# All tiles in SBUF on multiples of 64 bytes: a bias tile and a carried tile widened, 32 bytes left out at the upper end

## The chip, the cores and the metric

The kernel runs on one core of a Trainium2 chip. The metric is the device time of one execution in microseconds; three runs of the kernel before gave 2819.92, 2820.65 and 2821.26 us. A profile of one execution comes with it: for each engine (PE is TensorE, DVE is VectorE, ACT is ScalarE, POOL is GpSimd, SP issues most of the DMAs) each instruction's start and duration, and what released it when it had waited.

## The reference

A Fourier layer over 8 sequences of 3008 positions with 256 channels, followed by a gated feed-forward network over all 24,064 tokens:

```python
X = np.fft.rfft(x, axis=1)
Yr = Xr @ w_r - Xi @ w_i + b_r
Yi = Xr @ w_i + Xi @ w_r + b_i
Yr = np.sign(Yr) * np.maximum(np.abs(Yr) - lam, 0.0)   # lam = 0.01
Yi = np.sign(Yi) * np.maximum(np.abs(Yi) - lam, 0.0)
y = np.fft.irfft(Yr + 1j * Yi, n=x.shape[1], axis=1)
...
gate = 1.0 / (1.0 + np.exp(-(y @ w_gate)))
return gate * (y @ w_val) @ w_out                      # 256 -> 1536 -> 256
```

## The kernel before

**Staging.** The transform is split into two steps with 47 and 64 points. For each batch, `fwd_a` (its matmul is line 176) does the first step, its result goes through DRAM, `fwd_b` (line 237) does the second, `mix` or `mix4` (lines 271 and 293) multiplies by the complex weights, `inv_b` (lines 305 to 310) begins the inverse, again through DRAM, and `inv_a` (line 340) ends it. The feed-forward network then runs in two ways. The first nine chunks of 512 tokens go one after another: for each of 12 blocks of the hidden width, `ffn1` (lines 399 to 401) makes gate and value, and `ffn2` (lines 427 to 429), two blocks behind, multiplies by `w_out`. The FFT of the later batches is done between these units. The other tokens are taken in 19 pairs of 512 after the last FFT; for them the first layer is done by a scheme with seven products in place of eight (`product`, line 659), and `second` (lines 634 to 636) does the last layer. One pass through `half` has seven such products, three matmuls each, and one hidden block of `second` for both halves of the pair, twelve matmuls.

**Operands.** Most matmuls take float32 values as a high part and a low part of fewer bits: `yth` and `ytl` are the two parts of the transform's result for a chunk, `hh` and `hl` those of the gated hidden values, `w1h` and `w1l` those of the first layer's weights, and `w2` holds both parts of the last layer's. A product is then three matmuls (high by high, low by high, high by low). In a row of the profile, `po<-hh,w` means the result `po` from the moving operand `hh` and the stationary weights `w`.

**Memory.** Tiles come from pools that lie on two stacks in each partition of SBUF. From the left: `const` (`fb_sb`, `w1h`, `w1l`, `w2`), `cw` (`fa_sb`, `w_sb`, `bias_sb`, `ebias`), and `p2` (the FFT's working tiles, such as `xsh`, `xsl`, `yh`, `yl`, `zf`, `mi_sb` and, at the start, the warm-up tile `zero`). When the FFT is over, `cw` and `p2` are closed, and `p4` takes their place: `th` and `tl` (weights of the seven-product scheme), ten slots `xop` for its moving operands (`a11`, `s1` and so on; three of them serve as `spare` for the last hidden blocks of the first nine chunks), `ypair` and `sop`. From the right: `p0` (first batch), in whose place comes `p3` (`vf`, `yth`, `ytl`, `carry`, `sg`, `hh`, `hl`, and `ry` for results), in whose place comes `p5` (temporaries `tmp`, the hidden parts `hp`, results `ot2`). A pool's tiles stand one behind the other, and each tile takes a multiple of 32 bytes. The tile `carry` holds what `inv_a` computes beyond the end of a chunk until the next one begins; `ebias` is a column of one constant that ScalarE adds while the weights, given as 64-bit floats, are brought to 32 bits.

In the program before, `const` starts at byte 16,512 of a partition and the right stack ends at byte 229,344. `ebias` is the last tile of `cw`, at 105,472 and 32 bytes wide, so `p2` starts at 105,504. `carry` is 1504 bytes wide, at 205,312; right of it stand `sg`, `hh`, `hl` and `ry`, left of it `ytl`, `yth` and `vf`.

**Order.** The start is written out by hand up to the end of the twelve first units; after that the side work is put between units by weights. No queue and no order is touched by the change.

Of the kernel before, what the change touches and what calls it, by code (L numbers as in the profile page):

```python
# [9 lines left out]
F32 = mybir.dt.float32  # L10
# [99 lines left out]
def tile_fft_mix_ffn(ctx: ExitStack, tc, x, w_r, w_i, b_r, b_i, w_one, w_out, mf, mi, mis, fa, fb, out):  # L110
# [3 lines left out]
    P = 128  # L114
    XR = x.shape[2]
    CT = D // P
# [4 lines left out]
    UT = 2 * PT  # L121
# [6 lines left out]

    const = ctx.enter_context(tc.tile_pool(name="const", bufs=1))

    p0s = ExitStack()
    p0 = p0s.enter_context(tc.tile_pool(name="p0", bufs=1, side="right"))
    p3s = ExitStack()
    fft = ExitStack()
    cw = fft.enter_context(tc.tile_pool(name="cw", bufs=1))
# [5 lines left out]
    def bank(name, tag="fft", bufs=FFT_BANKS):  # L141
        return (psf if tag == "fft" else psl).tile([P, 512], F32, tag=tag, bufs=bufs, name=name)
# [185 lines left out]
    def split_y(c, at, n, y):  # L328
        if c not in yts:
            yts[c] = [p3.tile([P, CT, CW], F32R, name=t) for t in ("yth", "ytl")]  # L330
        yh, yl = (t[:, :, at:at + n] for t in yts[c])
        nc.scalar.copy(yh, y)
        sub(yl, y, yh)

    def inv_a(u):
        vf = held.pop(("v", u))
        pa = bank("pia")[:, :CT * UT].rearrange("p (c h k) -> p c h k", c=CT, h=2)
        for hh in range(2):
            for ct in range(CT):
                nc.tensor.matmul(pa[:, ct, hh], vf[:, hh, ct * P:(ct + 1) * P], fb_sb[:, :PT], start=True, stop=True)  # L340
        py = pa.rearrange("p c h k -> p c (h k)")
        lo = u * UT
        n = 0
        if lo < T0:
            c, at = divmod(lo, CW)
            n = min(UT, CW - at)
        if 0 < n < UT and lo + n < T0:
            t = p3.tile([P, CT, UT], F32, name="carry", bufs=1)[:, :, :UT - n]
            nc.scalar.copy(t, py[:, :, n:])
            held["carry", c + 1] = t, UT - n  # L350
        if n:
            split_y(c, at, n, py[:, :, :n])
        if lo + UT > T0:
            t = result("yf")
            t = t[:, :CT * (UT - n)].rearrange("p (c k) -> p c k", c=CT)
            nc.scalar.copy(t, py[:, :, n:])
            nc.sync.dma_start(yd[:, :, lo + n - T0:lo + UT - T0], t)

    def result(name):
        return p3.tile([P, CW], F32, tag="ry", bufs=NYF, name=name)  # L360
# [123 lines left out]
    def ffn_units():  # L484
        units, todo = [], {}
        seq = [(c, f) for c in range(NPL) for f in range(NF)]

        def own(c):

            return range(-(-c * CW // UT), -(-(c + 1) * CW // UT))  # L490

        for c in range(1, NPL):
            at = (c - 1) * NF
            for i, u in enumerate(own(c)):
                todo.setdefault(at + (0, 3, 6)[i], []).append(lambda u=u: load_v(u))
                todo.setdefault(at + (3, 6, 9)[i], []).append(lambda u=u: inv_a(u))
            todo.setdefault(at + 1, []).append(lambda c=c: carry(c))

        def unit(n):
            c, f = seq[n]  # L500
            if n == 0:
                for i, u in enumerate(own(0)):
                    if i == 1:
                        w = w1h[:, 0].rearrange("p i t n -> p (i t n)")
                        keep_warm(bank("warm", "l1", L1_BANKS), w[:, :P], w, WARM_V)
                    inv_a(u)
            ffn1(c, f)
            for t in todo.pop(n, ()):
                t()
            if n >= LAG and n - LAG < len(seq) - BEHIND:  # L510
                ffn2(*seq[n - LAG])
        return [lambda n=n: unit(n) for n in range(len(seq))], own(0), own(NPL - 1)[-1] + 1
# [228 lines left out]

    bias_sb = cw.tile([P, 2, D], F32, name="bias_sb")
    bias4 = p0.tile([P, D], F32, name="bias4")
    ebias = cw.tile([P, 1], F32, name="ebias")
    fb_sb = const.tile([2 * NQ, P], F32, name="fb_sb")
    w1h = const.tile([P, NF, 2, CT, P], F32R, name="w1h")
    w1l = const.tile([P, NF, 2, CT, P], F32R, name="w1l")
# [183 lines left out]
    p3 = p3s.enter_context(tc.tile_pool(name="p3", bufs=2, side="right", reuse_waits="tile"))  # L931
# [18 lines left out]
    def inverse(g):  # L950

        us = [u for b in g for u in range(b * H // 2, (b + 1) * H // 2) if u >= u0]
        ahead = min(NVF - 1, len(us))

        def begin():
            for u in us[:ahead]:
                load_v(u)

        def go(i):
            if i + ahead < len(us):  # L960
                load_v(us[i + ahead])
            inv_a(us[i])
        return [(0.0, begin)], [(0.65, lambda i=i: go(i)) for i in range(len(us))]

    def behind(g):

        loads, units = inverse(g)
        return (loads, 0.05, 0.05), (units, 0.1, 1)

    def merge(*streams):  # L970

        return [u for _, _, u in sorted(((lo + (hi - lo) * (i + 0.5) / len(s), k, u) for k, (s, lo, hi) in
                                         enumerate(streams) for i, u in enumerate(s)), key=lambda t: t[:2])]

    (a3, q3), (a4, q4) = (fft_units(g, {}) for g in groups[3:])
    n = len(a3) // 3
    side = (merge((second_fft, 0, 1), (a3[:n], 0.2, 1)) +
            merge((third_fft, 0, 1), (a3[n:], 0, 0.85), *behind(groups[1])) +
            merge((q3, 0, 1), (a4, 0, 0.85), *behind(groups[2])) +
            merge((q4, 0, 1), *behind(groups[3])))  # L980
# [9 lines left out]
    for j in range(NF, len(ffn)):  # L990
        c, f = divmod(j, NF)
# [39 lines left out]
    a, b, c, d = banks[0]  # L1031
# [4 lines left out]
    with tc.manual_schedule():  # L1036
        for k in range(2 * NPR * NH):
            p, e = divmod(k, 2 * NH)
# [18 lines left out]
        n = NPR * NH  # L1057
# [36 lines left out]
```

## Time and profile before

| | |
|---|---|
| median of three runs | 2820.65 us |
| span of the profiled execution, first to last instruction | 2819.0 us |
| TensorE busy | 2802.4 us |
| VectorE busy | 2082.3 us |
| ScalarE busy | 1309.6 us |
| GpSimd busy | 710.5 us |
| moved by DMA | 241.01 MB, 85 GB/s over the span |

The profile gives the profiled execution's own time as its span. It is one execution; the runs were taken without a profile, and their median is 1.65 us more than the span.

A row of the groups gives the line, the engine, the operation, output and inputs by the program's names, the shape of the tile, and the count; behind the first bar the busy time of the group in us and the mean duration of one in ns; behind the second the time that the engine was idle just before these instructions, and what ended most of it. Matmuls overlap: the next one starts before the last one is out, so a matmul that is said to take 389 ns follows the one before it at a shorter step. The time of a row of matmuls is read from the difference of two starts in the timeline.

### The profile page before, as it was taken

The page shows a single profiled execution, that of the slowest core. Times are in us where ns is not written, and L with a number is a line of the kernel's source. Part 1 is how long each engine was busy: PE and PEld are TensorE (multiplying, and loading weights), DVE is VectorE, ACT ScalarE, POOL GpSimd, SP SyncE. Part 2 cuts the span into 40 slices and gives each one's busy share as a digit, 9 for nine tenths or more (in the row PEclk, how much of TensorE's full clock was granted, in tenths as well). Part 3 has the DMA queues.
Part 4 walks back from the last instruction along what each step waited for, and adds up shares of the span by engine and source line. Part 5 has one row for each costly group of instructions (what it writes and reads, how often), then busy time and mean ns, then how long its engine had stood idle before and what let it go on. Part 6 is the DMA issues. An engine that isn't in the chain of part 4 may idle for free.

```text
span 2819.0 us, 38251 instructions
## 1 busy us (share of the span) xinstructions
PE 2802.4 (99%) x13896; PEld 2308.1 (82%) x13896; DVE 2082.3 (74%) x3109; ACT 1309.6 (46%) x2276; POOL 710.5 (25%) x638
## 2 busy tenths in 40 slices
PE   9999999999999999999999999999999999999999
PEld 6678888888899888888888888888888888888887
DVE  5777778667787536777777777777777777777776
ACT  4664544545455444444444444444444444444443
POOL 0211010224100002333333333333333343333321
PEclk9999999999999999999999999999999999999999
DMA  9866544666554661000000000000000000000000
GB/s 296 257 213 194 170 143 149 199 184 192 165 152 140 186 187 38 30 15 16 30 31 27 4 31 31 31 16 15 31 30 16 15 30 31 30 1 30 30 16 15
DMA packets 173469, 241.01 MB, mean 85 GB/s; under 512 B 14592, under 2 KB 124896, under 8 KB 173280
## 3 DMA queue, kind: packets, MB, share of 16 engines
q1 hardware_dynamic: 163776, 214.93, 24.8%
q0 software_dynamic: 9408, 23.60, 2.5%
q8 instruction: 110, 1.80, 0.3%
q14 instruction: 79, 0.65, 0.1%
q10 hardware_dynamic: 96, 0.04, 0.0%
HBM read 134.17 MB, written 104.33 MB: 85 GB/s over the span
## 4 chain that ended last, share of the span: by engine, by line
PE 94%; DVE 2%; DMA 2%; ACT 1%; issue 0%; SPq 0%; DVEq 0%; ACTq 0%
PE pd L659 11%; PE pa L659 11%; PE pc L659 11%; PE po L636 8%; PE po L635 8%; PE po L634 8%; PE pm L271 6%; PE pb L659 5%; PE pia L340 4%; PE pb L237 3%; PE pa L176 2%; PE pg L399 2%; PE pg L401 2%; PE pg L400 2%; PE pv L399 2%; PE pv L400 2%
## 5 line engine op out<-in xcount | busy, mean ns | idle before, releaser
L636 PE MATMUL po<-hl,w 128*128 128x512 f32 x912 | 362.5, 397 | 0.0
L635 PE MATMUL po<-hh,w 128*128 128x512 f32 x912 | 361.5, 396 | 0.0
L634 PE MATMUL po<-hh,w 128*128 128x512 f32 x912 | 360.8, 396 | 0.0
L718 POOL TENSOR_TENSOR c<-c,c 128x512 f32<-128x512 f32 x114 | 147.7, 1296 | 831.0 <-DVE c L714 640.1
L659 PE MATMUL pa<-a,w1h 128*128 128x512 f32 x912 | 284.0, 393 | 0.0
L659 PE MATMUL pc<-s,w1h 128*128 128x512 f32 x912 | 283.7, 392 | 0.0
L714 DVE TENSOR_TENSOR c<-u,pc 128x512 f32<-128x512 f32 x228 | 156.7, 687 | 114.7 <-PE pc L659 106.2
L689 DVE TENSOR_TENSOR u<-u,pb 128x512 f32<-128x512 f32 x228 | 155.3, 681 | 88.8 <-PE pb L659 62.6
L606 ACT CAST hh<-v 128x512 fp32r<-128x512 f32 x114 | 70.7, 620 | 306.2 <-DVE v L699 306.2
L636 PEld LDWEIGHTS po<-hl,w 128*128 128x128 f32 x912 | 171.5, 188 | 41.9
L634 PEld LDWEIGHTS po<-hh,w 128*128 128x128 f32 x912 | 172.0, 189 | 40.9
L635 PEld LDWEIGHTS po<-hh,w 128*128 128x128 f32 x912 | 171.0, 188 | 40.8
L659 PEld LDWEIGHTS pa<-a,w1h 128*128 128x128 f32 x912 | 171.2, 188 | 40.1
L659 PEld LDWEIGHTS pc<-s,w1h 128*128 128x128 f32 x912 | 171.0, 188 | 37.6
L610 POOL TENSOR_TENSOR hl<-c,hh 128x512 fp32r<-128x512 f32 x114 | 152.4, 1337 | 186.1 <-ACT hh L606 186.1
L271 PE MATMUL pm<-w_sb,xsh 128*128 128x256 f32 x1008 | 189.4, 288 | 1.4 <-ACT xf L177 1.1
L659 PE MATMUL pc<-s,w1l 128*128 128x512 f32 x456 | 177.5, 389 | 0.0
L659 PE MATMUL pa<-a,w1l 128*128 128x512 f32 x456 | 177.0, 388 | 0.0
L720 DVE TENSOR_TENSOR u<-u,pd 128x512 f32<-128x512 f32 x228 | 156.9, 688 | 24.5 <-DVE c L714 0.9
L693 DVE TENSOR_TENSOR v<-v,pc 128x512 f32<-128x512 f32 x228 | 156.6, 687 | 24.4 <-DVE v L691 0.5
L691 DVE TENSOR_TENSOR v<-u,pd 128x512 f32<-128x512 f32 x228 | 156.9, 688 | 24.0 <-DVE u L689 0.5
L685 ACT COPY u<-pa 128x512 f32<-128x512 f32 x228 | 133.7, 586 | 78.7 <-PE pa L659 78.6
(174 smaller groups left out, 6738.7 us busy)
## 6 DMA issues: line engine op xcount, KB each, us to landing
zf<-zd SPq DMA_DIRECT2D x96, 256.0 KB, 3.6
vf<-vd SPq DMA_DIRECT2D x128, 192.0 KB, 3.1
out_dram<-ot SPq DMA_DIRECT2D x93, 256.0 KB, 2.2
vd<-vz SPq DMA_DIRECT2D x84, 256.0 KB, 2.9
ypair<-yd SPq DMA_DIRECT2D x19, 1024.0 KB, 5.0
yd<-yf SPq DMA_DIRECT2D x103, 188.0 KB, 3.0
xf<-in_x_dram SPq DMA_DIRECT2D x48, 384.0 KB, 4.1
zd<-xf SPq DMA_DIRECT2D x44, 384.0 KB, 3.4
```

What stands on the lines that cost most here:

```text
L271: nc.tensor.matmul(o, l, r, start=(i == 0), stop=(i == len(mms) - 1))
L610: sub_(hl, h, hh)
L634: nc.tensor.matmul(o, wh, hh, start=(f == 0), stop=False)
L635: nc.tensor.matmul(o, wl, hh, start=False, stop=False)
L636: nc.tensor.matmul(o, wh, hl, start=False, stop=(f == NF - 1))
L659: nc.tensor.matmul(o, l, r, start=not more and l is wh and r is xh, stop=l is wl, skip_group_check=more)
L689: add(u, u, b)
L691: add(v, u, d)
L693: add(v, v, c)
L714: add(c12, u, c)
L718: nc.gpsimd.tensor_mul(c12, g12, c12)
L720: add(u, u, d)
```

## The change

Three edits, all in the sizes of tiles. A pool `edge` is opened on the right before all others and holds one tile of 8 floats (32 bytes), which nothing uses. `carry` is allocated with 384 floats (1536 bytes) in a partition in place of 2 x 188 (1504), and the old shape is taken as a view of it. `ebias` is allocated with 16 floats (64 bytes) in place of one, and its first column is used.

```diff
     const = ctx.enter_context(tc.tile_pool(name="const", bufs=1))
 
+    edge = ctx.enter_context(tc.tile_pool(name="edge", bufs=1, side="right"))
+    edge.tile([P, 8], F32, name="edge")
     p0s = ExitStack()
     p0 = p0s.enter_context(tc.tile_pool(name="p0", bufs=1, side="right"))
...
         if 0 < n < UT and lo + n < T0:
-            t = p3.tile([P, CT, UT], F32, name="carry", bufs=1)[:, :, :UT - n]
+            t = p3.tile([P, 3 * P], F32, name="carry", bufs=1)[:, :CT * UT].rearrange("p (c k) -> p c k", c=CT)[:, :, :UT - n]
             nc.scalar.copy(t, py[:, :, n:])
...
     bias4 = p0.tile([P, D], F32, name="bias4")
-    ebias = cw.tile([P, 1], F32, name="ebias")
+    ebias = cw.tile([P, 16], F32, name="ebias")[:, :1]
     fb_sb = const.tile([2 * NQ, P], F32, name="fb_sb")
```

## The prediction

> **What bounds the kernel.** I read the page first: span, busy shares, granted clock, the shares of the chain that ended last.
>
> ```profile
> span 2819.0 us, 38251 instructions
> ...
> PE 2802.4 (99%) x13896; PEld 2308.1 (82%) x13896; DVE 2082.3 (74%) x3109; ACT 1309.6 (46%) x2276; POOL 710.5 (25%) x638
> ...
> PEclk9999999999999999999999999999999999999999
> ...
> PE 94%; DVE 2%; DMA 2%; ACT 1%; issue 0%; SPq 0%; DVEq 0%; ACTq 0%
> ```
>
> TensorE is busy for 2802.4 of 2819.0 us at a granted clock of nine tenths or more in every slice, and it is 94% of the chain. All waiting together is 16.6 us. So the time moves only if matmuls follow each other faster, or if part of that 16.6 us goes. Next, the table by stage: stages cut at the end of the first FFT work, at the last FFN units and at the start of the long second part (lines 634 to 659).
>
> ```profile
> 0.00:120.00 120.00, 111.68 (x597) 0.99 0.90 278
> 120.00:450.00 330.00, 327.79 (x1855) 1.00 0.63 186
> 450.00:960.00 510.00, 508.28 (x3283) 1.00 0.55 166
> 960.00:1085.00 125.00, 124.99 (x682) 1.00 0.59 178
> 1085.00:2819.00 1734.00, 1729.64 (x7488) 1.00 0.07 23
> ```
>
> Columns are stage, length, TensorE busy (matmuls), granted clock, DMA share, GB/s. Half of the 16.6 us lies in the first 120 us, where the DMA share is 0.90; the last stage is 1734 us, TensorE alone, DMA at 0.07.
>
> **Part 1: what the change moves.** It adds and removes no instruction. I laid out both versions from the sizes in the code and the allocation of the program before, where the first constant tile starts at byte 16,512 of a partition and the right side ends at 229,344 = 3583 x 64 + 32. On the left, `ebias` takes 64 bytes instead of 32, so all tiles of `p2` go from 32 past a multiple of 64 to a multiple, up by 32. On the right, `edge` takes the top 32 bytes: `p0`, `p5` and the `sg`, `hh`, `hl`, `ry` part of `p3` move down by 32, onto multiples. `vf`, `yth` and `ytl` lay on multiples already; the wider carry tile and `edge` move them down by 64. `const`, the large tables of `cw` and all of `p4` stay. The gap between the sides shrinks from 1504 to 1408 bytes, so it fits.
>
> **Part 2: waits.** A pool that takes over another's bytes makes its tiles wait for those it overlaps. I compared the pairs `p4` over `cw`/`p2`, `p3` over `p0` and `p5` over `p3`: shifts of 32 bytes change no pair, since each boundary of one list keeps its side of the nearest boundary of the other. So no wait is added or taken away, nothing new queues behind anything, and no DMA is moved past another on SP's or POOL's queue. I price the waits at 0.
>
> **Part 3: the matmuls.** If addresses matter, the rows of equal matmuls from differently placed tiles must differ. These are 128x512 groups, shapes kept apart (last columns: busy us, mean ns, idle):
>
> ```profile
> L636 PE MATMUL po<-hl,w 128*128 128x512 f32 x912 | 362.5, 397 | 0.0
> L635 PE MATMUL po<-hh,w 128*128 128x512 f32 x912 | 361.5, 396 | 0.0
> L634 PE MATMUL po<-hh,w 128*128 128x512 f32 x912 | 360.8, 396 | 0.0
> ...
> L400 PE MATMUL pv<-ytl,w1h 128*128 128x512 f32 x216 | 85.5, 396 | 0.0
> ...
> L427 PE MATMUL po<-hh,w 128*128 128x512 f32 x210 | 84.8, 404 | 0.0
> ...
> L427 PE MATMUL po<-spare,w 128*128 128x512 f32 x6 | 2.3, 389 | 0.0
> ```
>
> The last two are the same line, weights and kind of bank; only the moving tile differs: `hh` lies 32 past a multiple of 64, `spare` (in `p4`) on one. 404 holds waits, but lines 634 to 636 wait for nothing and stand at 396 to 397. So the place of the moving tile goes with some 7 ns. The timeline shows what that costs in a row; start in us stands first. One of the 228 halves of the last stage (912 / 4):
>
> ```profile
> 2793.96 0.40 PE L634 MATMUL po<-hh,w 128*128 128x512 f32 x1
> ...
> 2796.78 0.63 PE L659 MATMUL pa<-a,w1h 128*128 128x512 f32 x2
> ...
> 2798.85 0.62 PE L659 MATMUL pa<-a,w1h 128*128 128x512 f32 x2
> ...
> 2801.57 0.40 PE L634 MATMUL po<-hh,w 128*128 128x512 f32 x1
> ```
>
> Twelve matmuls on `hh` and `hl` take 2796.78 - 2793.96 = 2.82 us, 235 ns from start to start. Twelve from `p4` later in the same half take 2801.57 - 2798.85 = 2.72 us, 226.7 ns. The nine in between (2.07 us, 230 ns) read `p4` too and come back to the short step only by and by. A half takes 7.61 us; 33 steps of 226.7 ns would be 7.48. The most that is to be had here is 228 x 0.13 = 29.6 us.
>
> The last FFN units, without side work:
>
> ```profile
> 1068.95 0.40 PE L427 MATMUL po<-hh,w 128*128 128x512 f32 x1
> ...
> 1069.65 0.39 PE L399 MATMUL pg<-yth,w1h 128*128 128x512 f32 x1
> ...
> 1072.45 0.63 PE L659 MATMUL pa<-a,w1h 128*128 128x512 f32 x2
> ```
>
> Twelve on `yth`/`ytl` take 2.80 us against 2.72: 0.08 x 108 units = 8.6 us. Three on `hh`/`hl` take 0.70 against 0.68: 0.02 x 2 x 105 = 4.2 us. With the last stage that makes a ceiling of 42.4 us.
>
> Now which property of the place it is. `yth` and `ytl` start on multiples of 64 (188,928 = 2952 x 64) and still step at 233 ns. And the warm-up tile `zero`, in `p2`, 32 past a multiple, in its last matmuls:
>
> ```profile
> L836 PE MATMUL warm<-zero x5: 388/389/393, 29.6 to 30.5; 128*128 128x512 f32 x5
> ```
>
> Least, median and longest: 389, the short value, off a multiple of 64. So the rows speak twice against "a multiple of 64 is what counts". Two properties fit all five tiles. (a) Distance to the weights, modulo 512: weight slices start at 128 past a multiple of 512, the operands of `p4` too (127,616), and `zero` is its own weight: distance 0, short. `yth` starts 128 short of that phase, `hh`/`hl` 160: long. After the change all of these stand at 192, a distance no 512-wide row shows. (b) Place in the partition: the long ones lie above 180,000, the short ones end at 168,576; nothing crosses over. Under (b) the change does nothing; under (a) it leaves distance 0 to the same tiles as before, and the new 192 is nearer to 160 and 128 (both long) than to 0 or 512. I take 0 for the sum, with -42.4 as the near end and a dearer pattern, below, as the other.
>
> The Trainium skill, page "SBUF — State Buffer", section "Door 1: The DMA port swizzle (why [64,N] ≈ [32,N])", says that SBUF has 16-byte lines and that crossing to a new one costs; tiles on multiples of 32 begin on such a line before and after, so by that rule alone the matmul term is 0, yet it leaves the 389 against 396 unexplained.
>
> **Part 4: the 256-wide matmuls of the FFT**, operands in `p2` and `cw`:
>
> ```profile
> L271 PE MATMUL pm<-w_sb,xsl 128*128 128x256 f32 x504 | 141.4, 281 | 0.0
> ...
> L293 PE MATMUL pm<-wi_sb,xsl 128*128 128x256 f32 x48 | 13.5, 281 | 0.0
> L293 PE MATMUL pm<-w_sb,xsl 128*128 128x256 f32 x48 | 13.4, 280 | 0.0
> ```
>
> `w_sb` lies on a multiple of 64 and `wi_sb` 32 off; they differ by 1 ns. Bounds: 1512 (line 271) x 1 ns = 1.5 us either way; I take 0.
>
> **Part 5: other engines and DMA.**
>
> ```profile
> L610 DVE TENSOR_TENSOR hl<-v,hh 128x512 fp32r<-128x512 f32 x114 | 79.0, 693 | 78.2 <-ACT hh L606 78.2
> ...
> L606 ACT CAST hh<-v 128x512 fp32r<-128x512 f32 x114 | 70.7, 620 | 306.2 <-DVE v L699 306.2
> ...
> L585 ACT CAST a<-ypair 128x512 fp32r<-128x512 f32 x57 | 34.9, 612 | 0.5 <-DMA ypair<-yd 0.5
> ...
> L416 DVE TENSOR_TENSOR spare<-sg,spare 128x512 fp32r<-128x512 f32 x3 | 2.1, 693 | 2.1 <-ACT spare L415 2.1
> ```
>
> VectorE takes 693 ns from tiles all 32 off and 693 where two of three are on a multiple; ScalarE 620 off against 612 on. At 46% ScalarE sits before it casts (306.2 us idle), so 8 ns times 456 casts, 3.6 us, lies beside TensorE's products: 0 on the path; if the cover went, 3.6 us at most. DMA: in the chain the longest piece is the first load of x.
>
> ```profile
> 3.18 10.38 DMA xf<-in_x_dram
> 13.57 8.18 DMA wf<-in_w_r_dram
> 21.83 7.47 DMA zd<-xf
> 33.16 6.18 DMA zf<-zd
> ```
>
> Together 32.2 us of transfers into or out of tiles that move by 32. No row shows the same load at both places, so bounds: 0, or a tenth of these 32.2 us, 3.2 us, either way; I take 0, as rows of 1 to 4 KB per partition are long against 32 bytes.
>
> Sum: 0 + 0 + 0 + 0 on a span of 2819.0 us. The median of the runs is 2820.65, 1.65 above the span; I keep that difference: 2820.7 us.
>
> **Rivals.**
> - *Distance 192 is as good as 0* (reading (a) with luck): every matmul of part 3 steps at 226.7 ns, -42.4 us, 2778 us. For: the sharp, exactly repeated short step. Against: 128 and 160 are both long. Chance 0.22.
> - *A multiple of 64 does count for `hh` and `hl`* and `yth` is long for a reason of its own: 29.6 + 4.2 = 33.8 us, 2787 us. For: `spare` against `hh` in line 427. Against: `zero` at 389. Chance 0.16.
> - *Slower: distance 192 gives a dearer pattern.* The dearest that recurs is line 636, most often 399 ns:
>
> ```profile
> L636 PE MATMUL po<-hl,w x912: 394/399/399, 1094.9 to 2814.6; 128*128 128x512 f32 x183
> ```
>
> If every 512-wide matmul on a moved tile took 399: 2736 x 2.7 ns on lines 634 to 636 = 7.4 us, 1296 x 3 on `yth`/`ytl` (396 on line 400) = 3.9, 630 x 3 on lines 427 to 429 = 1.9; 13.2 us, 2834 us. Its place is TensorE's operand reads; it decides from 5.6 us / 4662 matmuls = 1.2 ns each. Against: the mean is already 396. Chance 0.12.
> - *The change misses its aim* (a pool rounds its start, so that the tiles keep their places): 2820.7, within the forecast's case.
>
> **How the numbers follow.** No change (2815 to 2826, within 0.2%, about what a measurement of this kernel can tell from none): 0.50. Faster: 0.22 + 0.16 = 0.38. Slower: 0.12. The two faster cases are too likely to leave out, so the range reaches to 2777; above it ends at 2832, short of the full dearer pattern. That leaves about 0.1 out.
>
> **What would show it.** In the profile after: lines 634 to 636 stay at 394 to 399 and the half at 7.6 us if the forecast holds; 389 and 7.48 us under the first rival, with `yth` at 389 too; 389 there but `yth` at 393 to 395 under the second; 399 or more under the third. Lines 271 and 293 within 1 ns, the idle total near 16.6 us, no new releaser among TensorE's waits, else part 2 is wrong. I am wrong if the 512-wide means move by more than 1.2 ns without any of these patterns.

## The result, and the profile after

The changed kernel takes 2804.28 us (median of four runs, 2803.84 to 2806.39) against 2820.56 us before: ratio 0.9944, 95% interval 0.993 to 0.9958. It is 16.3 us faster, where no change was forecast, and inside the range. The page of the profiled execution (2804.69 us) begins so:

```profile
span 2802.9 us, 38251 instructions
...
PE 2786.4 (99%) x13896; PEld 2304.7 (82%) x13896; DVE 2084.6 (74%) x3109; ACT 1311.1 (47%) x2276; POOL 713.1 (25%) x638
...
PE 96%; DVE 2%; DMA 1%; ACT 0%; issue 0%; SPq 0%; DVEq 0%; ACTq 0%
```

The instructions are the same in number. TensorE idles for 2802.9 - 2786.4 = 16.5 us, as before (16.6). So the waits together are as long as before; the matmuls themselves follow each other faster. Two lines came in above, so every line number is 2 higher: 636 to 638 are the second layer of the last stage, 661 the seven products, 401 to 403 the first layer, 273 the mix products. The groups of the page, mean ns in the last column but one:

```profile
L636 PE MATMUL po<-hh,w 128*128 128x512 f32 x912 | 360.1, 395 | 0.0
L638 PE MATMUL po<-hl,w 128*128 128x512 f32 x912 | 358.0, 393 | 0.0
...
L637 PE MATMUL po<-hh,w 128*128 128x512 f32 x912 | 355.9, 390 | 0.0
...
L661 PE MATMUL pa<-a,w1l 128*128 128x512 f32 x456 | 179.2, 393 | 0.0
```

395, 390 and 393 stand where 396, 396 and 397 stood: neither the old 396 nor the short 389. And `pa<-a,w1l`, whose tiles did not move, has gone up; its row in the same groups of the kernel before, where 388 stands for 393:

```profile
L659 PE MATMUL pa<-a,w1l 128*128 128x512 f32 x456 | 177.0, 388 | 0.0
```

A stretch of the timeline of the changed kernel shows both:

```profile
2780.67 0.63 PE L661 MATMUL pa<-a,w1h 128*128 128x512 f32 x2
...
2782.76 0.62 PE L661 MATMUL pa<-a,w1h 128*128 128x512 f32 x2
...
2785.48 0.40 PE L636 MATMUL po<-hh,w 128*128 128x512 f32 x1
...
2788.24 0.40 PE L661 MATMUL pa<-a,w1h 128*128 128x512 f32 x1
```

The twelve on `hh` and `hl` take 2788.24 - 2785.48 = 2.76 us (2.82 before), the twelve products ahead of them 2.72 (as before), the nine products behind such a block 2.09 (2.07 before): part of the gain is given back right there. Over the 225 such blocks of the last stage the twelve take 2.814 us on average before and 2.763 after, the nine 2.078 and 2.085. The last unit of the first nine chunks:

```profile
1062.37 0.39 PE L401 MATMUL pg<-yth,w1h 128*128 128x512 f32 x1
...
1065.12 0.63 PE L661 MATMUL pa<-a,w1h 128*128 128x512 f32 x2
```

Twelve on `yth` and `ytl` take 2.75 us (2.80 before), although these tiles lay on multiples of 64 before as well.

By stage, from starts: the seven-product scheme begins at 1065.12 us (1072.45 before), and the last matmul starts at 2798.3 (2814.6 before):

```profile
L638 PE MATMUL po<-hl,w x912: 392/392/397, 1087.6 to 2798.3; 128*128 128x512 f32 x183
```

So the last stage went from 1742.2 to 1733.2 us, 9.0 us less, and all that lies ahead of it gained 7.3 us. Together that is the 16.3.

### The profile page after: what moved, and what is told of

Read it like the earlier page. It is cut to its first block, busy times and chain, and to the rows that moved or that the text cites. A ratio compares the mean times of both kernels' runs of the same rounds, so it can differ in the third digit from the quotient of the medians.

```text
span 2802.9 us, 38251 instructions
## 1 busy us (share of the span) xinstructions
PE 2786.4 (99%) x13896; PEld 2304.7 (82%) x13896; DVE 2084.6 (74%) x3109; ACT 1311.1 (47%) x2276; POOL 713.1 (25%) x638
## 4 chain that ended last, share of the span: by engine, by line
PE 96%; DVE 2%; DMA 1%; ACT 0%; issue 0%; SPq 0%; DVEq 0%; ACTq 0%
PE pd L661 11%; PE pa L661 11%; PE pc L661 11%; PE po L636 8%; PE po L638 7%; PE po L637 7%; PE pm L273 6%; PE pb L661 5%; PE pia L342 4%; PE pa L178 3%; PE pb L239 3%; PE pg L401 2%; PE pg L403 2%; PE pg L402 2%; PE po L429 2%; PE pv L401 2%
```

## The experiments

Where a mean step or a mean over blocks is given below, it is worked out from the starts of the matmuls in the trace. Three theories were set against each other. **Alignment**: a tile that starts on a multiple of 64 bytes is read faster. **Distance**: what counts is the start of the weights less the start of the moving operand, modulo some hundred bytes; 0 is short. **Place**: tiles in the upper part of the partition are slow. Below, a distance is given modulo 256 where nothing else is said; on the right side `hh` and `hl` stood at 160 before and `yth` and `ytl` at 128, and the change puts all four at 192.

**Distance 0 on multiples of 64.** One number is changed in the changed kernel:

```diff
-    edge.tile([P, 8], F32, name="edge")
+    edge.tile([P, 88], F32, name="edge")
```

> The changed kernel with 352 bytes left out at the upper end instead of 32, so that yth, ytl, hh, hl stay on multiples of 64 and start at 128 past a multiple of 512, as the weights do (distance 0). Distance theory (what counts is the start of the weights less the start of the moving operand, modulo 512): the 512-wide matmuls all step at 226.7 ns, a half takes 7.48 us plus the short DVE waits, lines for po at 389 ns, and the time is 2820.6 - 42 + 0 to -3 for the FFT: 2775 to 2782 us. Alignment theory (a multiple of 64 is what counts): all tiles were on one already, so 2804 us as after the change, po at 390 to 395. Place theory (upper part of the partition): also 2804.

Measured: 2784.51 us, ratio 0.9875 (0.986 to 0.989), and the groups of the second layer:

```profile
L636 PE MATMUL po<-hh,w 128*128 128x512 f32 x912 | 354.9, 389 | 0.0
L638 PE MATMUL po<-hl,w 128*128 128x512 f32 x912 | 354.8, 389 | 0.0
L637 PE MATMUL po<-hh,w 128*128 128x512 f32 x912 | 354.8, 389 | 0.0
```

A half of its timeline, nine products, twelve products and a block of twelve of the second layer:

```profile
2760.51 0.62 PE L661 MATMUL pa<-a,w1h 128*128 128x512 f32 x2
...
2762.55 0.62 PE L661 MATMUL pa<-a,w1h 128*128 128x512 f32 x2
...
2765.27 0.39 PE L636 MATMUL po<-hh,w 128*128 128x512 f32 x1
...
2767.99 0.62 PE L661 MATMUL pa<-a,w1h 128*128 128x512 f32 x2
```

From 2760.51 to 2767.99 that is 7.48 us, the ceiling of the prediction: the nine products behind the block take 2.04 us now, so their slowness was an after-effect of the block. Alignment and place both said 2804; both fall. The time is 2.5 us above the upper end of what distance gave. One reason is in the idle time at the products' line that VectorE ended, the first row of the kernel before, the second of this one (us in total, times):

```profile
  DVE u L720: 3.6, 10
```

```profile
  DVE u L722: 9.1, 24
```

These rows count weight loads and matmuls together; the matmuls' own idle time is 0.4 and 0.9 us of it. What it costs shows in the starts: in the last stage the matmuls that begin more than 245 ns after the one before them lose 1.8 us in total before and 5.0 us here, 3.2 us more. TensorE now comes early to some of VectorE's sums.

**Distance 0 off multiples of 64.** Everything that the feed-forward part reads is put 32 past a multiple:

```diff
-    edge.tile([P, 8], F32, name="edge")
+    edge.tile([P, 80], F32, name="edge")
...
+    const.tile([P, 8], F32, name="front")
     fb_sb = const.tile([2 * NQ, P], F32, name="fb_sb")
```

> The changed kernel with 32 bytes put in front of the constants and 320 left out at the upper end: every tile of the FFT, the weights, xop, yth, hh lies 32 past a multiple of 64, while the distance of weights and moving operand is 0 in the whole feed-forward part and 64 at line 273's products as after the change. Distance theory: same as with distance 0 on multiples of 64, 2775 to 2782 us. Alignment theory: all gain lost and xop's products slower too: 2821 us or more (4788 matmuls of the seven products at 396 in place of 389 ns would add some 25 us: 2845).

Measured: 2785.13 us, ratio 0.9877 (0.9863 to 0.9892).

```profile
L636 PE MATMUL po<-hh,w 128*128 128x512 f32 x912 | 354.9, 389 | 0.0
...
L661 PE MATMUL pa<-a,w1h 128*128 128x512 f32 x912 | 280.7, 389 | 0.0
```

389 in all these rows, with not one of these tiles on a multiple of 64. At distance 0 a multiple of 64 is not needed.

**The two sides alone.** Right: the change without the wider `ebias`. Left: the kernel before with the wider `ebias` and nothing else.

> The change without the wider bias column: p2 stays 32 past a multiple of 64 (distance 32 at the mix products), the right side as after the change. Both theories give the feed-forward part's share of the gain: of the 16.3 us, the step sums of the traces give 2736 x 4.25 ns = 11.6 us less for the second layer of the last stage, some 2 us given back by the seven products, and 3 to 4 us for the first nine chunks, so 2806 to 2808 us. If the mix products' 2 ns (1512 x 1.9 = 2.9 us) is real, the rest of the gain, about 3 us, is missing here.

> The kernel before with the wider bias column alone: p2 on multiples of 64, the right side as before. Expected 2820.6 less about 3 us for the mix products (116.3 in place of 118.2 ns from start to start, 1512 of them): 2817 to 2818 us, half and feed-forward rows as before (7.61 us, po at 396 to 397). If the FFT part gains nothing: 2820.6.

Measured: right side 2806.94 us, 0.9955 (0.994 to 0.997), 13.4 us less than before; left side 2815.47 us, 0.9984 (0.9974 to 0.9994), 4.9 us less. They add up to 18.2 us, where the whole change gave 16.3; the intervals do not tell the two apart. The left side's gain is nearer 5 than 3. On it, the mix products moved from distance 32 to 64; the three rows are those of the left side alone, of the right side alone, and of the whole change:

```profile
L271 PE MATMUL pm<-w_sb,xsl 128*128 128x256 f32 x504 | 140.1, 278 | 0.0
```

```profile
L273 PE MATMUL pm<-w_sb,xsl 128*128 128x256 f32 x504 | 141.0, 280 | 0.0
```

```profile
L273 PE MATMUL pm<-w_sb,xsl 128*128 128x256 f32 x504 | 140.6, 279 | 0.0
```

281 stood there before. Such means hide how soon the next matmul follows. From start to start (steps over 140 ns, which hold waits, left out) the mix products take 118.2 ns before and 115.4 with the left side alone; 1512 x 2.8 ns = 4.2 us, most of the 4.9. The matmuls of line 176, whose distance the same edit moves from 96 to 64 in most of them, keep their median step of 429 ns. In the whole change the step is 116.3 ns at the same distance of 64, and over all kernels with that distance it goes from 114.4 to 116.5 ns, though only the right side differs between most of them: distance does not set it alone.

**Which distances.** The same edit with other widths: 24 floats left out give distance 256, 72 give 448 (192 modulo 256).

> The changed kernel with 96 bytes left out at the upper end instead of 32: yth, ytl, hh, hl at 384 past a multiple of 512, distance 256 to the weights. If the distance counts modulo 256 (or less): short steps as at distance 0, 226.7 ns, about 2784 us. If modulo 512 and falling off with the distance from 0: at 192 the step in a row is 229.0, at 160 it is 233.3, so 256 would go on falling, 226.7 to 229, 2784 to 2800 us. If 192 was a dip: 230 ns or more, over 2805 us.

> The changed kernel with 288 bytes left out at the upper end: distance 448, that is 64 short of 512. If only distances from about 100 to 200 cost (one stretch of the 512): 226.7 to 227 ns, 2784 to 2787 us. If every distance but 0 costs, by how near it is: steps of 230 ns or more, 2805 us or more.

Measured, one run each: 2784.73 and 2805.21 us. 256 is as good as 0, and 448 is the same as 192, so the period is 256 or a part of it, and a distance 64 short of a whole period is not cheap. (The points at 32, 64 and 128 below leave no part of 256 that is a multiple of 32.)

**The cost put where it was not.** In the kernel with distance 0, the operands of the seven products are moved to distance 192, still on multiples of 64 (and with them the three `spare` slots, which 18 matmuls of the second layer read):

```diff
                 th, tl = (p4.tile([P, NH, 2, 3, P], F32R, name=t) for t in ("th", "tl"))
+                p4.tile([P, 80], F32, name="between")
```

> The kernel with distance 0 and on 64, with 320 bytes put between tl and the operands of the seven products in p4, so that a11 to a22 start at 448 past a multiple of 512 (still multiples of 64): distance 192 to w1h, w1l, th, tl, where it was 0. Distance theory: the 4788 matmuls of the products go from 226.7 to about 229 to 230.5 ns from start to start, as po did at that distance after the change: 11 to 18 us more, less what the waits on VectorE take up: 2790 to 2803 us, po at 389. Alignment theory: no change, 2784.5 us.

Measured, one run: 2807.08 us, 22.6 us more than the kernel it was made from, 4 us beyond the upper end expected, and:

```profile
L661 PE MATMUL pa<-a,w1h x912: 388/394/398, 1063.8 to 2790.9; 128*128 128x512 f32 x183
...
L661 PE MATMUL pc<-s,w1h x912: 388/394/398, 1065.9 to 2791.6; 128*128 128x512 f32 x183
...
L661 PE MATMUL pa<-a,w1l x456: 392/392/397, 1064.3 to 2791.1; 128*128 128x512 f32 x152
```

Least, median, longest: medians of 392 to 394 where 389 stood. The second layer's twelve, still at distance 0, slowed as well, from 2.721 to 2.766 us on average over 225 blocks; they now follow products at 192. These 10 us were not in the estimate, and the price came out above it.

**The mix products at distance 0**: `ebias` 512 bytes wide in the kernel with distance 0.

> The kernel with distance 0 and on 64, with the bias column widened to 512 bytes in place of 64: p2 starts at a multiple of 512, and the mix products (line 273, moving w_sb, weights xsh and xsl) have distance 0 in place of 64. If the 256-wide products follow the same rule as the 512-wide: shorter steps, 1512 matmuls by 1 to 3 ns, 2780 to 2783 us. If a 256-wide product is bound otherwise (its steps were 118.6 ns at distance 0 in the inverse products): 116.3 to 118.6 ns, 2784.5 to 2788 us.

Measured: 2788.81 us, 0.9887 (0.987 to 0.9903): 4.3 us slower than with the mix products at 64.

```profile
L273 PE MATMUL pm<-w_sb,xsl 128*128 128x256 f32 x504 | 142.6, 283 | 0.0
```

From start to start the mix products take 119.6 ns in place of 116.3, 5.0 us over 1512. They do not follow the rule of the 512-wide: for them 0 is dear (a mean of 283 ns) and 64 cheaper (279).

**Multiples of 64 at other distances.** If the change was wrong in its reason, was it at least right that multiples of 64 help? On the right side, 120 floats left out give distance 128, 104 give 64, all tiles on multiples of 64.

> The changed kernel with 480 bytes left out at the upper end instead of 32: every tile lies on a multiple of 64, as after the change, but yth, ytl, hh and hl start at a multiple of 512, at distance 128 to the weights, where yth stood before the change. Distance theory (modulo 256): the steps on hh and hl in a row go back to 233 ns and yth to 232 to 233, so the feed-forward part's gain goes and only the FFT part's 5 us stays: 2813 to 2818 us. Alignment theory: 2804 us.

> The changed kernel with 416 bytes left out at the upper end: distance 64 to the weights on the right side. By the points so far (0: 226.7, 128 and 160: about 233, 192: 229.0 ns in a row) a curve even in the distance modulo 256 gives the 229 of 192 here: 2803 to 2807 us. If the cost begins only past some 100 bytes: 226.7 ns, 2784.5 us.

Measured: 2806.49 us, 0.9949 (0.9934 to 0.9964), and 2808.69 us. The first is a miss: 7 us below the least that distance gave, and near the 2804 of alignment. Its steps are as slow as expected; its products recover faster. A block and what follows it, at distance 128:

```profile
2787.98 0.40 PE L636 MATMUL po<-hh,w 128*128 128x512 f32 x1
...
2790.77 0.63 PE L661 MATMUL pa<-a,w1h 128*128 128x512 f32 x2
...
2792.83 0.40 PE L636 MATMUL po<-hh,w 128*128 128x512 f32 x1
```

The twelve take 2.79 us, 233 ns each, against 2.82 at distance 160, and the nine behind them 2.06 against 2.07 (on average over the blocks 2.791 against 2.814 and 2.056 against 2.078). The median steps behind a block are 232, 232, 231 and then 227 ns at 128; at 160 they are 233, 236, 224, 231, 236, 228, 232, 231 and only then 227. At the very end of the kernel, where 34 matmuls on `hh` and `hl` run with nothing between, the step is 233.4 ns at 128, 233.3 at 64 and 233.6 at 160. So distances alike in a row differ in what they do around a change of operands. For that reason the curve was filled: 128 bytes left out give distance 32, 192 give 96, 64 give 224, none 160; these lie 32 past a multiple of 64.

> The changed kernel with 128 bytes left out at the upper end: yth, ytl, hh, hl 32 past a multiple of 64, at distance 32 (modulo 256) to the weights, p2 as after the change. If a distance that is no multiple of 64 costs more than any that is: the last stage, from the first of the seven products to the last matmul, stays near the 1742 us of distance 160 (1733 to 1735 at 64, 128 and 192; 1716 at 0), 2812 to 2817 us. If the cost follows the distance from 0 step by step: between 0 and 64, 1716 to 1735 us, 2785 to 2808 us.

> As before with 192 bytes left out: distance 96, no multiple of 64. Multiple-of-64 distances cheaper as a class: last stage near 1742 us, 2812 to 2817 us. Step by step: as its neighbours 64 and 128, 1733 to 1736 us, 2804 to 2809 us.

> As before with 64 bytes left out: distance 224, no multiple of 64. Class: last stage near 1742 us, 2812 to 2817 us. Step by step: between 192 and 256, 1716 to 1733 us, 2785 to 2805 us.

> The changed kernel with nothing left out at the upper end: p2 on multiples of 64, and hh, hl, yth, ytl all at distance 160, where hh and hl stood before. It should come out as the left side alone, 2815 us, last stage 1742 us, by either theory; yth and ytl, now off the multiples of 64 and at 160 instead of 128, should step at 233 ns in a row as before.

All points, with the left side as after the change. Time is a median of four runs for 0, 128 and 192, one run for the others; the four runs of one kernel lie up to 4.5 us apart, so the last stage says more than the time. Last stage is the start of the last matmul less the start of the first product. Step is the mean over the last 33 starts.

| distance of `yth`, `ytl`, `hh`, `hl` | on a multiple of 64 | time, us | last stage, us | step at the end, ns |
|---|---|---|---|---|
| 0 | yes | 2784.5 | 1715.8 | 226.7 |
| 32 | no | 2809.7 | 1736.6 | 233.3 |
| 64 | yes | 2808.7 | 1735.3 | 233.3 |
| 96 | no | 2813.3 | 1735.1 | 234.2 |
| 128 | yes | 2806.5 | 1732.9 | 233.4 |
| 160 | no | 2820.8 | 1742.3 | 233.6 |
| 192 (the change) | yes | 2804.3 | 1733.2 | 228.9 |
| 224 | no | 2812.5 | 1739.1 | 233.4 |
| 256 | yes | 2784.7 | 1715.7 | 226.7 |

Only 0 (256) stands out. The rest lies between 2804 and 2821 us. Neither reading of these points holds as it was put: a class of multiples of 64 would have had 32 and 96 near 1742, and they are at 1736.6 and 1735.1; a curve that follows the distance step by step would have had 224 at or below the 1733 of 192, and it is at 1739.1. The last of the four missed as well: 2820.8 us in place of 2815. Its last stage is the expected 1742.3, so the rest lies ahead of it. In the profiled execution of the left side alone, itself at 2818.2 us, the first matmul of `ffn1` starts at 109.4 us, as here; from there to the first product it takes 960.4 us, here 962.9. The step of the `ffn1` matmuls (waits left out) is 232.1 ns there, at distance 128, and 233.4 here, at 160, some 1.7 us over 1296. What remains is within the spread of the left side's own runs, 2814.1 to 2819.5 us.

**A better version.** The kernel with distance 0, with 192 bytes put ahead of `yh` and `yl`, so that the inverse products go to 64 as well:

```diff
+        p2.tile([P, 48], F32, name="gap", bufs=1)
         for bh in beside[:NR2K]:
```

> The kernel with distance 0 and on 64, with 192 bytes put in p2 ahead of yh and yl, so that the inverse products (lines 310 to 312, 256 wide, moving yh and yl, weights mi) have distance 64 modulo 256 in place of 0. The mix products, 256 wide too, took 119.6 ns from start to start at distance 0 and 116.3 at 64; if the inverse ones do the same, 504 matmuls by 2 to 3 ns: 1.0 to 1.5 us less than 2784.5, within what the rounds can tell. The row to read is the step itself, 118 ns at distance 0.

Measured: 2784.38 us, 0.9871 (0.9854 to 0.9887): not to be told from the 2784.51 without it. The step that the expectation named went from 118.1 to 116.3 ns, near the 2 to 3 ns expected; that is 0.9 us over 504 matmuls, less than the four runs of this kernel differ (2782.0 to 2786.0 us). The row of line 312 went from 281 to 280 ns:

```profile
L312 PE MATMUL pi<-yh,mi_sb 128*128 128x256 f32 x168 | 47.0, 280 | 0.0
```

The kernel with 352 bytes left out, 2784.5 us, beats both the kernel before and the changed one; the gap adds nothing that can be measured.

## Why the prediction was wrong

**Parts 1 and 2 held.** The instruction count is the same and TensorE's idle time is 16.5 us for 16.6. The change is one of addresses alone.

**Part 3 read the rows rightly up to its last step.** Its case against a multiple of 64 (`yth` on one and slow, `zero` off one and short) is borne out: everything moved off multiples lost nothing at distance 0, and the products moved to distance 192 lost 22.6 us while they stayed on multiples. Of its two readings, place fell: with `hh` and `yth` still in the upper part, distance 0 gave short steps, 389 ns for `hh`. Distance was right, but with period 256, not the 512 in which it was written; 256 came out like 0.

**The step that failed** is the value taken for the new distance: "the new 192 is nearer to 160 and 128 (both long) than to 0 or 512. I take 0". 192 has a step of its own, 228.9 ns in a row, between 226.7 and 233.6. The last stage, a term put at 0, gained 9.0 us: each block takes 2.814 - 2.763 = 0.051 us less, 11.5 us over 225, of which the products behind them took back some 2.6, as the nine take 2.085 us for 2.078 and the twelve after those 0.004 more. The means of the three lines fell by 1, 6 and 4 ns, on average by more than 1.2, without any of the listed patterns, which is the prediction's own sign of being wrong. To go by the nearest measured distance was no sound rule: the table shows no order between 32 and 224, and 128 and 160, both long by their steps, differ by 9.4 us in the last stage. With two neighbours at one level, and no reason for a smooth course between them, the value should have stayed open between the ends, and the chance of no change below one half. That 2804 lies in the range is luck: the range was stretched down for two rivals at 2778 and 2787, and neither came.

**Part 4 was mis-sized.** It bounded the FFT's 256-wide products by 1.5 us from two rows 1 ns apart; the left side alone gained 4.9 us (1.7 to 7.3 by its interval). The two rows compared `w_sb` with `wi_sb` as an on and off of 64. By distance to `xsl` they stood at 32 and at 64, the old distance of line 271 and the one to come, and showed no gain. But line 293 takes three matmuls of each in turn, so neither distance lasts there; in line 271 the same move made the step 1.9 to 2.8 ns shorter. Why line 293 did not show it stays open.

**The first rival's** property was right and its place wrong: distance 0 does gain, but the change does not reach it. The 35.8 us of the kernel with distance 0 hold the left side's 4.9, so of the rival's 42.4 some 31 came. In the last stage it was 26.4 us of 29.6, and the longer waits for VectorE (3.2 us) are the rest. In the first nine chunks the term for `ffn1` was too large: 8.6 us were taken from the last unit, which has no side work, while the mean step of all 1296 matmuls (waits left out) went only from 232.5 to 229.6 ns, 3.8 us. **The second rival** (multiples of 64 count for `hh` and `hl`) fell with the result, as the change put both on one and their means stayed at 390 to 395, not 389; in the off-64 run they stood at 389 without one. **The slower rival** did not come: 192 is no dearer pattern, and no distance made the last stage longer than 160 did.

**Part 5** was not tested by itself. The start to the first matmul of `ffn1` goes from 106 to 110 us between the profiled executions, so its bounds of 3.2 and 3.6 us stay open.

**Still open**: why a distance costs at all; why distances with equal steps in a row differ by up to 9 us around changes of operands; and whether 160 and 224 are dear because they are no multiples of 64, as 32 and 96 are not. For the change itself this means: its last stage came out as that at 128, 1733 us for both, although the steps at the end are 228.9 and 233.4 ns, and 192 off a multiple of 64 was not run. So it is not shown whether the 9.0 us came by the new distance alone or also by `hh` and `hl` coming onto a multiple of 64.

## What to carry to other kernels

Where TensorE is the bound, compare equal matmuls whose operands lie in different pools; if their means differ with no wait between, look at the start of the weights less the start of the moving operand modulo 256, and for 512-wide matmuls bring it to 0: here that was one number in the changed kernel and 19.8 us more, 35.8 us in all. Rounding the starts of tiles up to multiples of 64 is no substitute: it moved the distance from one value other than 0 to another and got less than half of that. A price for a value that no row shows should not be taken from its neighbours unless rows show that the course between them is smooth.

## What the runs showed of the hardware that was not expected

A matmul's step depends on those before it. Behind a block of the second layer at another distance, nine products at distance 0 took 2.05 to 2.09 us on average (228 to 232 ns each); with the block at distance 0 they took 2.04. The steps are back at 227 ns after three when the block is at distance 128, after eight at 160 and after ten at 192, step for step within 2 ns in over 95% of the 225 blocks of each kernel.

The 256-wide mix products do better at another distance than the 512-wide matmuls: at 0 they have a mean of 283 ns, at 64 one of 279, and the kernel is 4.3 us slower with the former.

The Trainium skill, page "SBUF — State Buffer", section "Door 1: The DMA port swizzle (why [64,N] ≈ [32,N])", says that SBUF has 16-byte lines and that an access that crosses to a new one pays a penalty. Every tile that these matmuls read begins on a multiple of 32 in all these kernels, and the steps of equal matmuls still went from 226.7 to 234.2 ns; that rule gives no period of 256 bytes, and the measurement decides.
